# A four-layer attention and Fourier kernel: the feature transform of the spectral layers moved behind the sequence transform, in seven block products instead of eight

## The chip, the cores and the metric

The kernel runs on one core of one Trainium2 chip. The core has a matrix engine (TensorE, in the profile PE, its weight loads PEld), a vector engine (VectorE, DVE), a scalar engine (ScalarE, ACT), a general engine (GpSimd, POOL) and a queue engine that issues most of the transfers (SyncE, SP). Each engine works through its own instructions in order and waits for semaphores of the others. The metric is the time of one execution on the device in microseconds (us), the median of several runs.

## What is computed

Four residual layers over a sequence of 2,048 rows with 640 features, all in float32. Layers 0 and 2 are a local attention (32 heads of 20, each row sees 8 rows, itself and seven earlier ones two apart), layers 1 and 3 are a Fourier mixing whose two transforms are written as products with given matrices.

```python
def _B_ref(x, dft_seq_re, dft_seq_im, dft_hid_re, dft_hid_im):
    a = jnp.einsum("bsd,ed->bse", x, dft_hid_re)
    b = jnp.einsum("bsd,ed->bse", x, dft_hid_im)
    y = jnp.einsum("ts,bse->bte", dft_seq_re, a) - jnp.einsum("ts,bse->bte", dft_seq_im, b)
    return y

x = A_x
x = x + _A_ref(_layernorm(x, axis=-1), A_wqkv, A_wo)
x = x + _B_ref(_layernorm(x, axis=-1), B_dft_seq_re, B_dft_seq_im, B_dft_hid_re, B_dft_hid_im)
x = x + _A_ref(_layernorm(x, axis=-1), A_wqkv, A_wo)
x = x + _B_ref(_layernorm(x, axis=-1), B_dft_seq_re, B_dft_seq_im, B_dft_hid_re, B_dft_hid_im)
```

## The kernel before

**Precision.** Every operand of a matrix product is split in two float32r numbers, high and low, by a copy on ACT and a subtraction on DVE. A product is three passes (`PASSES`: high by high, high by low, low by high) into the same bank of PSUM, the accumulators. There are eight banks of 128 x 512, called `m0`, `m1`, `xt`, `t0`, `t1`, `pq`, `aux0` and `aux1`.

**The spectral layer** (class `LayerB`, line 902) applies the sequence transform first. The 2,048 output rows are eight tiles of 256. For a tile t, z = C x, where C has a real and an imaginary part side by side (512 columns) and x has 640 features: five blocks of 128 features, each one bank. The sequence matrix comes from DRAM in pieces of 128 x 512 ("tables", `cs`, 256 KB), sixteen to a tile, and is split as it comes. Then the feature transform makes y from z (`ymm`, line 1063): for 128 rows, five blocks of features, two halves of 320 output columns, three passes, real and imaginary: 60 products of 320 columns. Its weights, real and negated imaginary, are loaded and split in each spectral layer by `load_w` (line 1000) and stay in SBUF. `yout` (line 1082) adds the residual rows, stores them and, in layer 1, collects the statistics of the next layer's norm.

**Tiles 0 and 1** are made plainly, 15 products of 512 columns a table (`z_mm`, line 981): tile 0 at the end of the attention layer before, tile 1 at the start of the spectral layer (`zpart`, line 1024). Beside tile 1, DVE and ACT form sums and differences of blocks of x (`x_whole`, `x_combine`), which are stored to DRAM (`xcb`).

**Tiles 2 to 7** go in three pairs (`pair`, line 1179). The first 512 features are done by seven block products instead of eight (m1 to m7, each two banks, on sums and differences of quarters of the matrix and of x); the last 128 features plainly (f1, f2, one bank each). A pair takes three sweeps over eight table steps: m5, m4, m7 (18 products of 512 columns a step), then m2, f1, f2, m1 (21), then m3, f2, m6 (15). Each sweep reads its tables from DRAM again and splits them; kept operands of x come back by `x_slot`. Between sweeps DVE and ACT empty the banks and form z. The feature products of the previous tile stand between the sweeps of a pair, 60 at a time, those of the pair's first tile are strewn through the third sweep, 12 a step, and 60 stand after it.

**The way to the next attention layer.** `early` (line 601) runs the last pair of layer 1 with hooks that load, normalise and transpose the first rows of layer 2. The two halves of the last tile's feature products (`prev.ymm`, line 832) stand in steps -3 and -2 of attention's own hand-written order, among the first groups of its query, key and value product (g0 to g15, 15 products of 480 columns each; `LEAD2`, line 47, gives their steps). Keys and values of a group are stored to DRAM (`qkv_store`, line 385) and come back as windows; a query is copied by ACT into PSUM (`q_copy`, line 417); then attention's first product on DVE can start.

**Order.** In the attention layers the order of all engines is written out. In the spectral layers the order of PE alone is; the other engines' order, SP's too, is planned by the framework's scheduler. SP has at most eight transfers outstanding.

Of the kernel before, what the change touches and what calls it, by code (L numbers as in the profile page):

```python
# [20 lines left out]
D = 640  # L21
# [7 lines left out]
NJ = 4  # L29
# [49 lines left out]
XAPART = {(m, i) for i in range(2, NP - 2, 2) for m in (7, 1)}  # L79
# [7 lines left out]
def tile_layers(ctx: ExitStack, tc: tile.TileContext, x, wqkv, wo, cs, wre, wim, out):  # L87
# [29 lines left out]
    for tag, w in (("r1_0", D), ("pr0", D), ("win", SLOTS * FE)):  # L117
        T([P, w], tag, bufs=NWIN if tag == "win" else 1)
# [10 lines left out]
    xcb = [{m: dr.tile([P, NP, 2, 256], F32, name=f"xc_{l}_{m}") for m in XC} for l in range(2)]  # L129
# [126 lines left out]
    def layer_a(li, stats, handoff, prev):  # L256
# [344 lines left out]
        def early():  # L601
# [4 lines left out]
            def w0():  # L606
                with tc.issue_after(prev.dma.ins):
                    wq[0] = a_weights_q(0)

            def xt(j, part, bank="pq"):  # L610
                xt_pe(0, j, part, bank)
                xt_hi(0, j, part)
                xt_lo(0, j, part)

            prev.pair(
                NPAIR - 1,
                stats,
                {
                    2: lambda: (x_get(0), x_get(1)),
                    4: lambda: xt(0, 0),  # L620
                    5: lambda: x_get(2),
                    6: lambda: xt(0, 1),
                    7: lambda: (w0(), xt(1, 0), x_get(3)),
                    ("y", 0): lambda: xt(1, 1),
                    ("y", 1): lambda: (xt(2, 0, "xt"), xt(2, 1, "t0")),
                    ("y", 2): lambda: xt(3, 0),
                    ("y", 3): lambda: xt(3, 1, "xt"),
# [202 lines left out]
        if prev is not None:  # L830
            for j2 in range(2):
                at(j2 - 3, "pe3", prev.ymm, NT - 1, j2, 0, KD)
                at(j2 - 2, "actl", prev.yout, NT - 1, j2, stats)
# [68 lines left out]
    class LayerB:  # L902
        def __init__(self, li):
# [4 lines left out]
            self.zt = {}  # L908
            self.xl, self.raw, self.ct = {}, {}, {}
            self.xc = xcb[li // 2]  # L910
            self.whole = {}
            self.nraw = self.nhl = self.nx = 0

# [86 lines left out]
        def load_w(self):  # L1000
            self.wr = None
            self.wi = [None] * KD
            tags = ("stg", "stg", "xa", "xa")
            for n, (x, k) in enumerate([(x, k) for k in range(KD) for x in "ri"]):
                raw = T([P, D], tags[n] if n < 4 else "xa", bufs=2)
                nc.sync.dma_start(raw, (wim if x == "i" else wre)[:, k, :])
                if x == "i":
                    wt = T([P, 2, D], f"pr{k}" if k < 4 else "zo3", F32R)
                    self.wi[k] = wt[:, 0], wt[:, 1]
                    split(wt[:, 0], wt[:, 1], raw, neg=True)  # L1010
                else:
                    if self.wr is None:
                        self.wr = T([P, 2, KD, D], "r2a", F32R)
                    split(self.wr[:, 0, k], self.wr[:, 1, k], raw)

# [8 lines left out]
        def zpart(self, t, s0, s1):  # L1024
            for s in range(s0, s1):
                self.cw_load(t, s)
                self.c_hl(s, t)
                self.z_mm(s, None, t)

        def zt_new(self, t):  # L1030
            self.tt = [T([P, 5, 256], tg, F32R) for tg in ("zo0", "zo1", "zo2", "ot")]
            self.zt[t] = {}

        def zt_put(self, t, k, z):
            tt, zt = self.tt, self.zt[t]
            loc = [divmod(k * 4 + d, 5) for d in range(4)]
            for d in range(4):
                zt[(k, d // 2, d % 2)] = tt[loc[d][0]][:, loc[d][1]]
            pieces = [[], []]
# [6 lines left out]
            for o, r in pieces[0]:  # L1046
                nc.scalar.copy(o, z[:, r])
# [358 lines left out]
```

## Time and profile before

| | us |
|---|---|
| median of 3 runs | 1756.59 (1749.93 to 1758.09) |
| the profiled execution's own time | 1755.72 |
| its span in the trace | 1753.9 |
| PE busy | 1724.9 |
| DVE busy | 1372.8 |
| ACT busy | 804.9 |
| POOL busy | 627.9 |

The page gives for one execution the busy time of each engine, the span in 40 slices, the transfers, the chain of work that ended last, and the costliest groups of instructions. Views of the trace give groups of instructions by line, instructions in order of time, and busy times of each engine in chosen windows. In a row such as `12.34 0.39 PE L1171 MATMUL t<-r,r 128*128 128x512 f32 x3`, the first number is the start in us from the span's start, the second the time that the merged instructions took, then engine, source line, operation, output and inputs by the program's names, shapes and how many instructions the row merges. Matmuls are pipelined: a single one is shown with 0.3 to 0.4 us, while the next starts earlier, so that paces are read from start to start.

### The profile page before, as it was taken

The numbers are of one execution on the slowest core, as the hardware profiler recorded it, in microseconds if no ns is written. First come the engines' busy times: TensorE is split into PE (matmuls) and PEld (weight loads), VectorE is DVE, ScalarE is ACT, GpSimd is POOL, SyncE is SP. The second block draws the span as 40 slices with busy tenths as digits, with TensorE's granted clock in tenths as the row PEclk, the third lists the DMA queues.
The fourth block names the chain that finished last, engine by engine and source line by source line (L and its number), as shares of the span: only waits on it lengthen the run. The fifth ranks groups of instructions, "written<-read, shape, count | busy, mean of one in ns | idle before, by whom it ended". The sixth has DMA issues, their size and how long they took to land.

```text
span 1753.9 us, 26453 instructions
## 1 busy us (share of the span) xinstructions
PE 1724.9 (98%) x8798; PEld 1502.2 (86%) x8798; DVE 1372.8 (78%) x2127; ACT 804.9 (46%) x1683; POOL 627.9 (36%) x589
## 2 busy tenths in 40 slices
PE   9999999899999999999999999999999999999999
PEld 7888888788888888888898889988788888888888
DVE  6999999988767767767648999989777677677673
ACT  5664543554444444445534434444434443443441
POOL 4899999940000000000028998889200000000000
PEclk9999999999999999999999999999999999999999
DMA  8997769759787777686657866798597867767861
GB/s 285 309 314 217 227 200 335 260 185 313 260 264 243 242 258 231 233 278 221 198 178 237 267 205 214 220 326 278 192 316 254 262 209 253 260 220 237 261 205 53
DMA packets 273961, 426.20 MB, mean 243 GB/s; under 512 B 22656, under 2 KB 153728, under 8 KB 273568
## 3 DMA queue, kind: packets, MB, share of 16 engines
q1 hardware_dynamic: 270624, 422.54, 73.3%
q10 hardware_dynamic: 3200, 1.97, 0.4%
q8 instruction: 70, 1.15, 0.3%
q14 instruction: 67, 0.55, 0.1%
HBM read 339.28 MB, written 85.14 MB: 242 GB/s over the span
## 4 chain that ended last, share of the span: by engine, by line
PE 72%; DVE 11%; DMA 8%; POOL 4%; issue 3%; ACT 1%; SPq 0%; DVEq 0%; ACTq 0%; POOLq 0%
PE m L376 17%; PE aux L1074 14%; PE t L1171 10%; PE m L1171 10%; PE pq L1171 5%; PE xt L1171 5%; PE aux L529 5%; PE m L992 2%; DMA win<-kvb 2%; PE t L992 2%; DVE pr L445 2%; DVE pr L485 2%; DMA xc<-stg 1%; POOL pr L504 1%; DMA win<-cs_in 1%
## 5 line engine op out<-in xcount | busy, mean ns | idle before, releaser
L376 PE MATMUL m<-r,s 128*128 128x480 f32 x1920 | 435.7, 381 | 1.4 <-ACT stg L383 1.0
L376 PEld LDWEIGHTS m<-r,s 128*128 128x128 f32 x1920 | 355.0, 188 | 55.0 <-ACT stg L383 1.8
L1164 ACT CAST r<-win 128x512 fp32r<-128x512 f32 x246 | 149.8, 620 | 168.4 <-DVE win L1200 92.1
L1074 PE MATMUL aux<-r2a,zo 128*128 128x320 f32 x768 | 226.1, 309 | 0.0
L504 POOL TENSOR_TENSOR pr<-pr 128x640 f32<-128x640 f32 x126 | 207.0, 1643 | 33.9 <-DVE pr L485 33.8
L1074 PE MATMUL aux<-pr,zo 128*128 128x320 f32 x704 | 207.8, 309 | 0.0
L188 POOL TENSOR_TENSOR stats<-stats,mhalf 128x1 f32<-128x1 f32 (+1 forms) x40 | 28.5, 712 | 492.3 <-ACT stats L184 483.1
L445 DVE TENSOR_TENSOR pr<-pq,win 128x1280 f32<-128x1280 f32 x128 | 189.8, 1484 | 12.5 <-DMA win<-kvb 7.1
L1165 DVE TENSOR_TENSOR r<-win,r 128x512 fp32r<-128x512 f32 x246 | 165.6, 688 | 43.3 <-ACT r L1164 41.6
L485 DVE TENSOR_TENSOR pr<-pq,win 128x1280 f32<-128x1280 f32 x128 | 190.7, 1491 | 5.1
L448 POOL TENSOR_TENSOR pr<-pr 128x640 f32<-128x640 f32 x117 | 168.5, 1440 | 14.7 <-DVE pr L445 11.8
L1171 PE MATMUL m<-r,r 128*128 128x512 f32 x594 | 151.3, 389 | 0.3 <-DVE r L1165 0.3
L1074 PEld LDWEIGHTS aux<-r2a,zo 128*128 128x128 f32 x768 | 144.1, 188 | 1.9
L1074 PEld LDWEIGHTS aux<-pr,zo 128*128 128x128 f32 x704 | 132.2, 188 | 2.1
L1171 PE MATMUL t<-r,r 128*128 128x512 f32 x498 | 133.5, 390 | 0.0
L1171 PEld LDWEIGHTS m<-r,r 128*128 128x128 f32 x594 | 111.2, 188 | 23.6 <-DVE r L1165 0.9
L992 PE MATMUL m<-s,r 128*128 128x512 f32 x384 | 120.1, 400 | 8.3 <-DMA s<-c0b 5.5
L992 PE MATMUL t<-s,r 128*128 128x512 f32 x384 | 118.1, 396 | 0.2 <-DVE ot L1049 0.2
L455 DVE TENSOR_REDUCE lg<-pr 128x64 f32<-128x640 f32 (+1 forms) x128 | 111.4, 871 | 6.4 <-POOL pr L448 6.1
L505 POOL TENSOR_TENSOR pr<-pr 128x320 f32<-128x320 f32 x126 | 112.2, 890 | 9.9
L1171 PEld LDWEIGHTS t<-r,r 128*128 128x128 f32 x498 | 93.5, 188 | 20.0
L383 ACT COPY stg<-m 128x480 f32<-128x480 f32 x128 | 71.0, 555 | 84.4 <-PE m L376 63.4
(301 smaller groups left out, 3204.8 us busy)
## 6 DMA issues: line engine op xcount, KB each, us to landing
win<-cs_in SPq DMA_DIRECT2D x351, 256.0 KB, 3.8
r<-xc SPq DMA_DIRECT2D x240, 256.0 KB, 4.4
win<-kvb SPq DMA_DIRECT2D x96, 440.0 KB, 4.7
xa<-cs_in SPq DMA_DIRECT2D x121, 256.0 KB, 3.7
win<-kvb SPq DMA_DIRECT2D x64, 360.0 KB, 4.6
kvb<-stg SPq DMA_DIRECT2D x60, 320.0 KB, 5.2
xc<-stg SPq DMA_DIRECT2D x32, 512.0 KB, 4.3
s<-c0b SPq DMA_DIRECT2D x26, 512.0 KB, 5.2
```

Of the source, the lines that this page charges most:

```text
L376: nc.tensor.matmul(mt[g][:, : 3 * F], st[:, a, k], wq[q][:, b, k], start=n == 0, stop=n == 14)
L445: nc.vector.tensor_tensor(pr, q, wview(u, jp, 0, [[1, FE]]), op=ALU.mult)
L448: nc.gpsimd.tensor_tensor(pv[:, :, 0:10], pv[:, :, 0:10], pv[:, :, 10:20], op=ALU.add)
L455: nc.vector.tensor_reduce(lgs[u][:, :, 2 * jp : 2 * jp + 2].rearrange("p h j w -> p (j w) h"), prq.pop((u, jp)), axis=AX.X, op=ALU.add,)
L485: nc.vector.tensor_tensor(pr.rearrange("p j w (h d) -> p j w h d", d=DH), lgs[u][:, :, 2 * jp : 2 * jp + 2].rearrange("p h j w -> p j w h" ...
L504: g.tensor_tensor(pr[:, :, 0:4], pr[:, :, 0:4], pr[:, :, 4:8], op=ALU.add)
L505: g.tensor_tensor(pr[:, :, 0:2], pr[:, :, 0:2], pr[:, :, 2:4], op=ALU.add)
L992: self.last = nc.tensor.matmul(self.z[t][k], self.xn[c][:, a, j, k * P : (k + 1) * P], self.ct[s][:, b], start=s == 0 and i == 0, stop=s = ...
L1074: self.last = nc.tensor.matmul(self.ym[e][:, :320], zt[(k, a, ri)][:, j2 * P : (j2 + 1) * P], w[:, e * 320 : (e + 1) * 320], start=(k, a, ...
L1164: nc.scalar.copy(hi, raw)
L1165: nc.vector.tensor_tensor(lo, raw, hi.bitcast(F32), op=ALU.subtract)
L1171: nc.tensor.matmul(bank, w(a, kb), hl[b], start=start and (a, b) == (0, 0), stop=stop and (a, b) == (1, 0),)
```

## The change

All changes but names and buffers are in the two spectral layers and in the border from the first of them to the second attention layer.

1. **Feature transform last.** No feature product runs between or in the sweeps any more. Each tile's z is stored to DRAM (`zb`), five blocks of 128 x 512 a tile in pieces of 512 bytes, and read back by a last phase, `hid`, that does all eight tiles, two at a time.
2. **Seven block products of eight.** z (real and imaginary) has two by two blocks against the weights, by output half. `hid` forms seven operands from z for each tile (`prep`: 11 operations on DVE and 7 copies on ACT, on 128 x 640), three steps ahead of use, and multiplies each by one of seven operands made from the weights: 15 products of 320 columns an operand and tile, 210 for a pair of tiles in place of 240. Four pairs of banks take them; DVE adds eight bank halves a tile to the residual rows.
3. **Weights.** The seven weight operands are formed and split once, in layer 1's first sweeps (`b_prep`, 20 parts), stored to DRAM (`wbd`, 35 blocks of 320 KB) and read back by each layer's `hid`, as buffers come free: ten into `r2a`, four into `pr0` and `pr1` during the last second sweep, the rest around the start of `hid`.
4. **Two sweeps a pair.** With all eight banks free of feature products, a first sweep has m5, m2, m1, f1, f2 (30 products a step) and a second m3, m6, m4, m7 (24); m4 and m7 accumulate onto m2 and m1 in their banks.
5. **x operands.** Four of the five kinds of operands of x stay in SBUF, two of them written over the blocks of x that they replace; one (m1) goes through DRAM. For that, tile 1's tables are taken in another order.
6. **Border.** The hooks that load, normalise and transpose layer 2's first rows move into `hid`'s last two groups of tiles; attention's steps -3 to -1 hold no feature products.

```diff
-                m5, m4, m7 = banks("m0", "m1"), banks("xt", "t0"), banks("t1", "pq")
+                m5, m2, m1 = banks("aux0", "aux1"), banks("m0", "m1"), banks("t0", "t1")
+                f1, f2 = banks("xt"), banks("pq")
                 for i in range(NP):
...
+                    b22, b11, b21, b12 = raw(t2, NP + i), raw(t1, i), raw(t1, NP + i), raw(t2, i)
+                    x1 = self.x_slot(i)
+                    p22 = split(b22)
+                    self.product(m5, self.x_kept(5, i), p22, *ends)
+                    p11 = split(b11)
+                    self.product(m2, self.x_kept(2, i), p11, i == 0, False)
+                    c1 = comb(b22, b22, b11, ALU.add)
+
+                    self.product(m1, x1, c1, i == 0, False)
+                    self.product(f2, self.x_plain(*k2(i), 512), p22, i == 0, False)
+                    self.product(f1, self.x_plain(*k1(i), 512), p11, i == 0, False)
+                    p12 = split(b12)
+                    self.product(f2, self.x_plain(*k1(i), 512), p12, False, i == NP - 1)
+                    p21 = split(b21)
+                    self.product(f1, self.x_plain(*k2(i), 512), p21, False, i == NP - 1)
...
+                m3, m6 = banks("aux0", "aux1"), banks("pq", "xt")
+                for i in range(NP):
...
+                    c3 = comb(self.s_buf(tags), b12, b22, ALU.subtract)
+                    self.product(m3, self.x_plain(*k1(i), 0), c3, *ends)
+                    c6 = comb(b12, b11, b12, ALU.add)
+                    self.product(m6, self.x_kept(6, i), c6, *ends)
+                    c4 = comb(b11, b21, b11, ALU.subtract)
+                    self.product(m2, self.x_plain(*k2(i), 256), c4, False, i == NP - 1)
+                    c7 = comb(b22, b21, b22, ALU.add)
+                    self.product(m1, self.x_kept(7, i), c7, False, i == NP - 1)
+                    self.flush()
+                    if p == NPAIR - 1:
+                        self.hid_load(i)
...
+        def hid_load(self, i):
+            if i == 0:
+                self.b0 = self.b_tile("r2a", 0, 10)
+            if i in (0, 1, 2, 5, 6):
+                n = (0, 1, 2, None, None, 3, 4)[i]
+                self.b0(2 * n, 2 * n + 2)
+            if i == 4:
+                za = self.za_tile(0)
+                for n in range(2):
+                    za(n, 0, 4)
...
+        def hid_mm(self, t, n, bank, start, stop):
+            s = self.av.pop((t, n))
+            for k in range(KD):
+                w = self.wb[(n, k)]
+                for a, b in PASSES:
+                    nc.tensor.matmul(
+                        bank[:, :320],
+                        s[:, a, k],
+                        w[:, b],
...
+                for step in range(NT // 2 * NB):
+                    g, n = divmod(step, NB)
...
+                    for i, t in enumerate(ts):
+                        self.hid_mm(t, n, bank[which][i], n in (0, 1, 2, 4), n in (1, 2, 5, 6))
...
+                        for q in quarters:
+                            o = rows[(t, q // 2)][:, q % 2 * 320 : q % 2 * 320 + 320]
+                            v.tensor_tensor(o, bank[which][i][:, :320], o, op=ALU.add)
...
+                    self.prep(step + 3)
+                    if (g, n) in hooks:
+                        hooks[(g, n)]()
...
-        if prev is not None:
-            for j2 in range(2):
-                at(j2 - 3, "pe3", prev.ymm, NT - 1, j2, 0, KD)
-                at(j2 - 2, "actl", prev.yout, NT - 1, j2, stats)
```

562 lines of the change are left out of this document (306 added, 256 removed).

## The prediction

> **What bounds the kernel now.** I read the page's busy shares and its chain first, then the busy time by windows, then PE in order of time at both ends of each spectral layer.
>
> ```profile
> span 1753.9 us, 26453 instructions
> PE 1724.9 (98%) x8798; PEld 1502.2 (86%) x8798; DVE 1372.8 (78%) x2127; ACT 804.9 (46%) x1683; POOL 627.9 (36%) x589
> PE 72%; DVE 11%; DMA 8%; POOL 4%; issue 3%; ACT 1%; SPq 0%; DVEq 0%; ACTq 0%; POOLq 0%
> ```
>
> PE is busy nearly always, but a busy share says little about the pace. The windows do (columns: window, length, then busy us and instruction count of PE, PEld, DVE, ACT, POOL, then granted clock, DMA share, GB/s):
>
> ```profile
> 250.00:300.00 50.00, 46.51 (x246) 40.62 (x245) 46.74 (x70) 22.61 (x61) 46.16 (x43) 0.97 0.90 306
> 400.00:450.00 50.00, 49.97 (x248) 42.29 (x247) 39.51 (x59) 20.52 (x37) 0.00 (x0) 1.00 0.91 313
> 850.00:900.00 50.00, 50.00 (x299) 46.76 (x299) 21.93 (x41) 24.58 (x52) 5.04 (x4) 1.00 0.52 162
> 1050.00:1100.00 50.00, 50.00 (x280) 45.46 (x279) 45.95 (x72) 22.16 (x57) 45.08 (x43) 1.00 0.68 220
> 1150.00:1200.00 50.00, 46.64 (x245) 40.48 (x245) 43.13 (x67) 22.30 (x58) 44.49 (x43) 0.97 0.97 339
> 1400.00:1450.00 50.00, 50.00 (x256) 43.74 (x255) 37.53 (x63) 22.11 (x38) 0.00 (x0) 1.00 0.66 213
> ```
>
> In the spectral layers (400, 1400) POOL rests, DVE has 10 to 12 us of every 50 free, and PE has none. There the end is set by the number of products. In the attention layers (250, 1050) DVE and POOL are as full as PE. So this change is worth what it does to PE inside the spectral layers, and at their borders. The prices of a product come from start to start, since a product's own duration overlaps the next:
>
> ```profile
> 725.08 8.79 PE aux L1074 x60
> ...
> 1693.42 1.52 PE L1171 MATMUL m<-s,r 128*128 128x512 f32 x6
> 1694.78 0.39 PE L1171 MATMUL xt<-r,r 128*128 128x512 f32 x1
> ```
>
> Sixty feature products of 320 columns take 8.79 us on the chain, 0.1465 each. Six sequence products of 512 columns take 1694.78 - 1693.42 = 1.36 us, 0.2267 each.
>
> ```profile
> 401.30 0.30 PE L1074 MATMUL aux<-r2a,zo 128*128 128x320 f32 x1
> ...
> 902.50 7.76 PE L376 MATMUL m<-r,s 128*128 128x480 f32 x35
> ...
> 1272.60 0.30 PE L1074 MATMUL aux<-r2a,zo 128*128 128x320 f32 x1
> ...
> 1750.33 0.31 PE L1074 MATMUL aux<-zo,ot 128*128 128x320 f32 x1
> ```
>
> 401.30 and 1272.60 are the first feature products of the layers; four tables of tile 1 (60 products, 13.6 us) stand ahead of them, so tile 1 starts at 387.7 and 1259.0. The first layer's last feature product ends as group g5 of the next attention begins, 902.50. Its PE work: 1,536 sequence products (348.2), 960 feature products (140.6), five groups (some 16.5) and 20 transposes (some 2): 507 of 514.8 us, so about 7.5 idle. Layer two: 348.2 + 140.6 = 488.8 of 1750.5 - 1259.0 = 491.5, under 3 idle.
>
> **The change, part by part.** *Feature products.* Seven block products of eight: per pair of tiles 7 x 2 x 15 = 210 instead of 240, per layer 840 instead of 960. Removed: 240 x 0.1465 = **35.2 us**, all on the path. Same width and passes, so I take the same pace. *Sequence sweeps.* Products stay 54 per table step (18 + 21 + 15 before, 30 + 24 after): no gain. Input loads fall, 216 to 192 table loads and 120 to 24 loads of kept operands a layer. The two x halves rewritten in place wait for PE's last table, and ACT evacuates five banks behind that: by the next rows some five copies at 0.62, of which two to three products cover half. Bounds 0 and 4, I take 2.
>
> ```profile
> L1164 ACT CAST r<-win 128x512 fp32r<-128x512 f32 x246 | 149.8, 620 | 168.4 <-DVE win L1200 92.1
> L1165 DVE TENSOR_TENSOR r<-win,r 128x512 fp32r<-128x512 f32 x246 | 165.6, 688 | 43.3 <-ACT r L1164 41.6
> ...
> 1681.13 0.68 DVE L1265 TENSOR_TENSOR s<-m,s 128x512 f32<-128x512 f32 x1
> 1681.73 0.68 DVE L1266 TENSOR_TENSOR stg<-stg,xt 128x512 f32<-128x512 f32 x1
> ```
>
> *Borders of sweeps.* Before, 60 feature products (8.79) or products strewn through the third sweep covered the emptying of banks. After, five borders a layer stand bare. DVE's operations on 512 columns follow each other at 0.60 (1681.13 to 1681.73). The first product into a reused bank comes 18 products (4.1 us) after its last use in most cases, more than four DVE additions (2.4). In the built order one border of the first layer has six such operations ahead of a half that PE needs 1.4 us later: 3.6 - 1.4 = 2.2. Bounds 0 and 11 (2.2 at all five); I take 1 a layer.
>
> *Second sweep.* Eight DVE operations a step (four combinations, four low halves): 8 x 0.60 = 4.8 us against PE's 24 x 0.2267 = 5.44. Cost nothing, covered by 0.6 us a step and by up to eight halves of lead; the rival below prices it without.
>
> *Hand-over to the feature products.* In the last second sweep SP also loads 14 weight blocks and two tiles of z back from DRAM, 22 x 320 KB = 7.2 MB, beside 20 table pieces (5.2 MB) for steps 2 to 6: 12.4 MB. The row at 1150 moves 339 GB/s at a share of 0.97, so 37 us, and from the point where the first weight buffer is free to step 6 PE has about 38 us. But the z loads (1.3 MB each) can only start when PE has left the first x quarter after step 3, two steps (10.9 us) ahead of step 6; they take 2.6 MB / 339 = 7.7 us and a landing of some 3 to 4:
>
> ```profile
> win<-cs_in SPq DMA_DIRECT2D x351, 256.0 KB, 3.8
> ```
>
> Behind them stand step 6's tables, and on DVE the first feature operand's halves (which wait for the z) stand ahead of step 5's last two and of step 6. Tables at about 12.5, then combination, high and low half (0.6 + 0.6 + 0.7 and hand-offs): 14.5 to 15 against 10.9, so **4 us**; bounds 0 (if the z land as fast as a short load, 3.8) and 8 (if they move at the 213 GB/s of the 1400 row, 12.3 us). After the sweep 7.5 MB more must land in six feature steps of 4.4 us: 22 us of 26. I take 1.5 (0 and 6). Small single waits, as the second layer has now: 1.5. Together 2 + 1 + 4 + 1.5 + 1.5 = **10 us a layer**.
>
> *Feature phase.* DVE per group of two tiles: 22 operations on 640 columns (some 0.75, scaled from 0.60 at 512) and 16 additions on 320 (some 0.4): 23 us against PE's 210 x 0.1465 = 30.8. Operands are made three steps ahead. Hidden; without the lead the fullest step (6 us) would cost 1.6 four times a layer. Its row loads wait for row stores on the same SP queue, with eight to ten us to spare.
>
> *The last tile's feature products leave the next attention's start.* They covered, with g4, the way of the first keys through DRAM:
>
> ```profile
> 881.86 0.56 ACT L383 COPY stg<-m 128x480 f32<-128x480 f32 x1 [0.35 <-PE m L376]
> 882.46 0.36 ACTq L392 DMA_DIRECT2D kvb<-stg  x1
> ...
> 905.15 0.42 ACT L418 COPY pq<-qs 128x320 f32<-128x320 f32 x1
> ...
> 908.23 1.48 DVE L445 TENSOR_TENSOR pr<-pq,win 128x1280 f32<-128x1280 f32 x1
> ...
> 890.46 3.41 PE L376 MATMUL m<-r,s 128*128 128x480 f32 x15
> ...
> kvb<-stg ACTq DMA_DIRECT2D x4, 320.0 KB, 2.7
> ...
> win<-kvb SPq DMA_DIRECT2D x96, 440.0 KB, 4.7
> ```
>
> Now from g3's copy (881.86) to attention's first product on DVE (908.23) 26 us pass, since ACT's query copy (905.15) stands behind the last tile's statistics. After: four groups (13.6), copy 0.6, store 3.1, load 4.7, and 3 for issue and queueing: DVE starts 25 us after the last feature product (bounds 22 and 30). PE has by then done g0 to g6 in both versions, so the rest of the attention layer is the same. The weight quarters of q come in one at a time through the one free window buffer, while four hold result rows; the last is due just at the end, within the bound.
>
> **The sum.** First layer from tile 1's start to attention's first DVE product: before 908.2 - 387.7 = 520.5; after 348.2 + 840 x 0.1465 (123.1) + 2 + 10 + 25 = 508.3: -12.2. Second layer to the last product: before 491.5, after 471.3 + 10 = 481.3: -10.2. The tail (last product to end, 3.4) has the same add and store. Total -22.4 from the profiled execution's 1755.7: 1733.3; that execution is 0.9 below the median of the runs, so **1734 us**.
>
> **Rivals.** *All covers hold* (waits of 2 a layer): 1734 - 16 = 1718. For it: layer two now idles under 3 us. Against: bare borders. *Clock*: where PE idled 3.5 us in 50 (250) or 3.4 (1150), the clock stood at 0.97, a further 1.5 us; 24 us of waits in such lumps would lose 24 / 3.5 x 1.5 = 10: 1744. Against: they are mostly short. The Trainium skill, "TensorE: Matmul & The Clock Gate", Part 1, says an idle window of about 3.4 us halves PE's clock until a busy one has passed; by that rule only the hand-over and the attention's start would pay, and the trace agrees as far as 0.97 beside those idle times goes. *The change doesn't reach the end at the first layer*: the attention's start takes back its 12 us because keys or weights come late: 1746. *Transfers late, the slower side*: place the hand-over. At 220 GB/s (the row at 1050) 12.4 MB take 56 us, 18 late, and 7.5 MB take 34, 8 late: 26 a layer for the 5.5 counted, +41: 1775. It decides from about 11 us a layer, near 250 GB/s; the mean is 243 with free time in it, full-share rows give 313 to 349, which speaks against. Stores of z in 512-byte pieces, which no row has, push this way. *Second sweep bound by DVE*: operations at 0.69 plus 0.18 of waiting for ACT (43.3 / 246) make 6.9 us a step against 5.44, 11.7 a sweep, 9 behind the lead, six sweeps: 1734 + 54 = 1788. Against: 0.60 back to back.
>
> **Chances.** Forecast 0.58 (own range 1722 to 1748); covers hold 0.10; clock 0.08; first layer lost 0.06; transfers late 0.12; DVE 0.06. Half a per cent, about what can be told from no change, is 8.8 us: faster means below 1747.8. Forecast 0.56, covers 0.10, clock 0.06, first layer 0.04: 0.76. Within: 0.11 (edges, and transfers a little late). Slower: 0.13. The range 1720 to 1758 leaves out half of the covers case, DVE, and most of late transfers, about 0.2.
>
> **What would show it.** Feature products 1,680 at 0.146 to 0.147 start to start; gaps of some 4 us in each layer's last second sweep ended by DVE or a z load; under 2.5 us at sweep borders; attention's first DVE product 22 to 30 us after the last feature product. Waits over 11 us a layer, or a second sweep step over 5.9 us, would make the prediction wrong.

## The result and the profile after

| | before | after |
|---|---|---|
| median of 4 runs, us | 1753.26 (1749.12 to 1758.09) | 1728.87 (1725.96 to 1730.85) |
| profiled execution's own time | 1755.72 | 1728.94 |
| its span | 1753.9 | 1727.1 |

The ratio of the times is 0.9859, with an interval of 0.9824 to 0.9893. Forecast were 1734 us and a range of 1720 to 1758. The page of the changed kernel:

```profile
span 1727.1 us, 25610 instructions
PE 1690.0 (98%) x8558; PEld 1465.1 (85%) x8558; DVE 1439.9 (83%) x2215; ACT 828.0 (48%) x1677; POOL 629.6 (36%) x589
PE 52%; DVE 21%; DMA 12%; POOL 7%; issue 4%; ACT 3%; SPq 1%; ACTq 0%; DVEq 0%; POOLq 0%
```

PE has 240 products and 34.9 busy us less (1724.9 - 1690.0), DVE 67 us more. In the chain DVE rises from 11 to 21% and transfers from 8 to 12%: PE still sets the end, but more often on the word of another. Where, the windows show (columns as before):

```profile
450.00:500.00 50.00, 47.90 (x210) 39.38 (x211) 40.62 (x68) 26.99 (x50) 0.00 (x0) 1.00 0.87 303
500.00:550.00 50.00, 46.86 (x198) 36.10 (x196) 45.65 (x78) 23.65 (x42) 0.00 (x0) 1.00 0.87 287
700.00:750.00 50.00, 47.04 (x198) 37.77 (x197) 40.12 (x66) 22.64 (x38) 0.00 (x0) 0.97 0.86 305
1400.00:1450.00 50.00, 50.00 (x223) 41.40 (x222) 34.16 (x56) 23.94 (x41) 0.00 (x0) 1.00 0.69 221
1550.00:1600.00 50.00, 47.09 (x202) 37.14 (x201) 40.70 (x66) 22.48 (x37) 0.00 (x0) 1.00 0.83 300
```

At 0.2267 a product, 50 us hold 220. Layer two's middle (1400) has them. Layer one lacks 10 to 22 in three of these windows, layer two 18 in its last one, and in all four the transfers are at 0.83 or more.

The ends of the stages, in PE's and DVE's instructions in order of time (tile 1's first product in each spectral layer, the last feature products, attention's first product on DVE), first after, then the one row of before that the prediction had only worked back:

```profile
386.54 1.30 PE L990 MATMUL m<-s,r 128*128 128x512 f32 x5
...
874.77 2.22 PE L1358 MATMUL m<-r,ot 128*128 128x320 f32 x14
...
901.66 1.49 DVE L447 TENSOR_TENSOR pr<-pq,win 128x1280 f32<-128x1280 f32 x1
...
1245.44 1.29 PE L990 MATMUL m<-s,r 128*128 128x512 f32 x5
...
1721.61 2.36 PE L1358 MATMUL m<-r,ot 128*128 128x320 f32 x15
```

```profile
1257.72 0.96 PE L992 MATMUL m<-s,r 128*128 128x512 f32 x3 [1.45 <-DVE zo L1049]
```

The first layer's last feature product ends at 874.77 + 14 x 0.1467 = 876.8, the second's at 1721.61 + 15 x 0.1467 = 1723.8. Stage by stage, in us (before's first layer starts at 387.3 by its trace):

| stage | before | after | difference | forecast |
|---|---|---|---|---|
| up to tile 1 of layer one | 387.3 | 386.5 | -0.8 | 0 |
| tile 1 to attention's first DVE product | 520.9 | 515.1 | -5.8 | -12.2 |
| second attention layer, to tile 1 of layer two | 349.5 | 343.8 | -5.7 | 0 |
| tile 1 of layer two to the last product | 492.8 | 478.4 | -14.4 | -10.2 |
| tail | 3.4 | 3.3 | -0.1 | 0 |
| sum | | | -26.8 | -22.4 |

So the time came out within 5 us of the forecast, but its parts did not: the first layer gained half of what was said, and something that the change doesn't touch gained as much as that layer. Of the 5 us, 3 lie in the reference: the forecast took 1756.6 us for before, the median of three runs, and with a fourth run it is 1753.3. As a difference of medians the gain is 24.4 us, where 22.6 were forecast.

### The profile page after: what moved, and what is told of

It reads as the page before. It is cut to its first block, busy times and chain, and to the rows that moved or that the text cites. A ratio compares the mean times of both kernels' runs of the same rounds, so it can differ in the third digit from the quotient of the medians.

```text
span 1727.1 us, 25610 instructions
## 1 busy us (share of the span) xinstructions
PE 1690.0 (98%) x8558; PEld 1465.1 (85%) x8558; DVE 1439.9 (83%) x2215; ACT 828.0 (48%) x1677; POOL 629.6 (36%) x589
## 4 chain that ended last, share of the span: by engine, by line
PE 52%; DVE 21%; DMA 12%; POOL 7%; issue 4%; ACT 3%; SPq 1%; ACTq 0%; DVEq 0%; POOLq 0%
PE m L378 10%; PE aux L1125 4%; PE t L1125 4%; DVE pr L447 4%; PE m L1125 4%; PE m L1358 4%; PE aux L1358 3%; PE m L990 3%; PE t L1358 3%; PE t L990 3%; DVE pr L487 3%; PE pq L1125 3%; PE xt L1125 3%; PE aux L531 3%; POOL pr L506 2%
## 5 line engine op out<-in xcount | busy, mean ns | idle before, releaser
L450 POOL TENSOR_TENSOR pr<-pr 128x640 f32<-128x640 f32 x117 | 168.4, 1440 | 14.2 <-DVE pr L447 13.4
L990 PEld LDWEIGHTS t<-s,r 128*128 128x128 f32 x384 | 72.4, 189 | 15.8 <-ACT r L366 0.5
L531 PE MATMUL aux<-r2a,ot 128*128 128x320 f32 x540 | 84.9, 310 | 0.7 <-ACT s L366 0.5
L990 PEld LDWEIGHTS m<-s,r 128*128 128x128 f32 x384 | 71.6, 189 | 16.3 <-DMA s<-c0b 2.4
L465 ACT ACTIVATE lg<-lg 128x128 f32<-128x128 f32 x64 | 20.1, 314 | 134.5 <-DVE lg L476 134.2
L531 PEld LDWEIGHTS aux<-r2a,ot 128*128 128x128 f32 x540 | 81.2, 188 | 2.8 <-ACT s L366 0.7
L990 PE MATMUL xt<-s,r 128*128 128x512 f32 x192 | 72.5, 391 | 0.0
L508 POOL TENSOR_TENSOR zo<-pr 128x160 f32<-128x160 f32 x126 | 68.1, 540 | 9.9
L1114 ACT CAST zo<-win 128x512 fp32r<-128x512 f32 x83 | 51.4, 621 | 28.5 <-DVE win L1119 13.6
L1115 DVE TENSOR_TENSOR zo<-win,zo 128x512 fp32r<-128x512 f32 x83 | 57.0, 687 | 7.6 <-ACT zo L1114 7.5
L420 ACT COPY pq<-qs 128x320 f32<-128x320 f32 x64 | 27.5, 430 | 70.5 <-DVE pr L487 48.7
```

The source lines that it names most:

```text
L450: nc.gpsimd.tensor_tensor(pv[:, :, 0:10], pv[:, :, 0:10], pv[:, :, 10:20], op=ALU.add)
L531: nc.tensor.matmul(m[:, :320], oT[(c, j)][:, a, k], wo_s["w"][:, b, k, e * 320 : (e + 1) * 320], start=(i, k) == (0, 0), stop=(i, k) == (2 ...
L990: self.last = nc.tensor.matmul(self.z[t][k], self.xn[c][:, a, j, k * P : (k + 1) * P], self.ct[s][:, b], start=s == 0 and i == 0, stop=s = ...
```

## Where the first layer's gain went, as the trace shows it

Of the first layer's 490.3 us (386.54 to 876.8), 471.3 are products by the prediction's prices and some 2 transposes: 17 are lost, for 10 forecast. Of the second's 478.4, 7.1 are lost. The feature phase itself is as forecast:

```profile
1657.81 4.56 PE L1358 MATMUL m<-r,s 128*128 128x320 f32 x30
1662.21 2.36 PE L1358 MATMUL aux<-r2a,s 128*128 128x320 f32 x15
```

4.40 / 30 = 0.1467 a product. Some 12 of the first layer's 17 us stand at three places (2.3, 4.4 and 5.1 us); the rest are losses of 1.1 us or less, at the second pair's middle, in the second sweeps and in tile 1. First, the middle of the first pair, between its two sweeps (rows of ACT, PE, SP and DVE in order of time; the bracket is the idle time ahead and what ended it):

```profile
497.37 0.74 ACT L142 ACTIVATE pr<-pr 128x640 fp32r<-128x640 f32 x1 [2.54 <-DMA wbd<-pr]
...
499.04 0.57 ACT L1248 COPY zo<-pq 128x512 f32<-128x512 f32 x1
...
499.67 0.96 PE L1125 MATMUL pq<-stg,r 128*128 128x512 f32 x3 [2.10 <-ACT zo L1248]
...
493.87 0.41 SPq L1103 DMA_DIRECT2D win<-cs_in  x1
499.64 0.52 SPq L1013 DMA_DIRECT2D zb<-zo  x1
...
505.94 0.38 SPq L1103 DMA_DIRECT2D xa<-cs_in  x1
...
511.33 0.69 DVE L1119 TENSOR_TENSOR win<-win,xa 128x512 f32<-128x512 f32 x1 [4.19 <-DMA xa<-cs_in]
```

An operation that forms the feature weights (L142) waits on ACT for the store of the block before it, and the bank copy that PE needs (L1248) stands behind it: 2.1 us on PE. SP stands from 493.87 to 499.64 at the store of that same copy, with tables behind it. A table of the second sweep is issued at 505.94, and DVE idles 4.19 us for it. From 511 on DVE runs without a gap: eight operations of 0.60 in a step of 5.44, and besides them, up to the border, eight operations of forming that take 4.2 us. Of a sweep's 43.5 us (eight steps) DVE so has about 1 free (43.5 - 64 x 0.60 - 4.2). Second, 30 us later, at the border to the next pair (PE):

```profile
540.76 0.39 PE L1125 MATMUL m<-zo,r 128*128 128x512 f32 x1
541.99 0.93 PE L1125 MATMUL aux<-e,r2a 128*128 128x512 f32 x3 [0.84 <-DVE s L1269]
544.39 0.94 PE L1125 MATMUL aux<-e,r2a 128*128 128x512 f32 x3 [1.47 <-DVE s L1269]
...
551.24 0.96 PE L1125 MATMUL t<-zo,xr 128*128 128x512 f32 x3 [0.24 <-DVE s L1277]
```

From 540.76 to 551.24 stand 27 products, worth 6.12: 4.4 us lost. The prediction had 2.2 at one border of this layer, which it doesn't name. Third, two steps into the last second sweep (SP, DVE, PE, and the busy times of ten us ahead of it and of four behind it):

```profile
697.42 0.80 SPq L1285 DMA_DIRECT2D r2a<-wbd  x2
...
700.32 0.92 SPq L1285 DMA_DIRECT2D r2a<-wbd  x2
...
704.18 0.34 SPq L1103 DMA_DIRECT2D e<-cs_in  x1
...
714.50 0.69 DVE L1119 TENSOR_TENSOR e<-e,win 128x512 f32<-128x512 f32 x1 [9.00 <-DMA e<-cs_in]
...
715.95 0.51 PE L1125 MATMUL aux<-stg,r 128*128 128x512 f32 x1 [2.24 <-ACT stg L1114]
717.18 2.32 PE L1125 MATMUL aux<-stg,r 128*128 128x512 f32 x5 [0.72 <-DVE stg L1115]
719.30 1.48 PE L1125 MATMUL pq<-ot,r 128*128 128x512 f32 x3
```

```profile
700.00:710.00 10.00, 10.00 (x46) 8.29 (x45) 5.50 (x10) 3.98 (x7) 0.00 (x0) 1.00 1.01 377
...
717.00:721.00 4.00, 3.82 (x10) 3.00 (x11) 4.00 (x8) 1.72 (x4) 0.00 (x0) 0.57 0.60 177
```

From 697.42 to 700.32 SP issues six transfers of two weight blocks each (640 KB, 3.8 MB). The transfers run at full share (1.01, 377 GB/s), and the table issued at 704.18 behind them reaches DVE 10.3 us later, where the page's medians for loads of a table are 3.1 to 4.1. PE waits 2.24 and 0.72, and then runs at half clock: five products take 2.12 us (717.18 to 719.30), not 1.13. Some 5 of the second layer's 7.1 us are lost in its last steps, in several waits of under 1 us, of which one is shown with what DVE did before it:

```profile
1564.99 0.69 DVE L1119 TENSOR_TENSOR win<-win,e 128x512 f32<-128x512 f32 x1 [6.90 <-DMA e<-cs_in]
...
1580.39 1.56 DVE L1331 TENSOR_TENSOR r<-r,r 128x640 fp32r<-128x640 f32 x2 [1.94 <-ACT r L1330]
...
1587.68 1.43 PE L1125 MATMUL aux<-pr,r 128*128 128x512 f32 x5 [0.72 <-DVE pr L1115]
```

Here DVE has the same late table (6.90), and then the first feature operand's halves (L1331), which wait for a load of z.

From this a theory: PE's waits in the sweeps are late tables, which DVE at 88% of a step (4.8 of 5.44) can't make up before the border. Against it stood the order at the border, the forming of weights, the number of buffers and the sheer bytes.

## The experiments

All are edits of the changed kernel. "Of before" is the ratio to the kernel before, run beside it (its median was 1751.8 to 1754.3). The last four columns are spans in the profiled execution: layer one from tile 1's first to the last feature product, from there to attention's first DVE product (the lead-in), from there to tile 1 of layer two, and layer two to its last product.

| run | median us (runs) | of before | layer one | lead-in | attention | layer two |
|---|---|---|---|---|---|---|
| changed kernel | 1728.87 (4) | 0.9859 | 490.3 | 24.8 | 343.8 | 478.4 |
| e1_again | 1729.16 (4) | 0.9863 | 490.4 | 25.6 | 344.1 | 477.6 |
| e2_no_forming | 1726.69 (4) | 0.9845 | 485.5 | 25.2 | 345.4 | 478.0 |
| e3_eight_views | 1727.85 (4) | 0.9855 | 486.9 | 24.5 | 344.2 | 480.1 |
| e4_eight_products | 1766.63 (4) | 1.0073 | 507.2 | 24.2 | 347.4 | 494.7 |
| e5_weights_spaced | 1724.08 (4) | 0.9839 | 485.2 | 25.1 | 345.9 | 475.8 |
| e6_first_quarter_first | 1730.34 (4) | 0.9876 | 491.0 | 26.7 | 344.0 | 477.3 |
| e7_one_order | 1734.16 (4) | 0.9896 | 492.7 | 24.6 | 345.2 | 478.9 |
| e8_forming_on_pool | 1747.83 (10) | 0.9969 | 507.5 | 24.0 | 344.7 | 478.1 |
| e9_stores_later | 1725.49 (4) | 0.9848 | 485.6 | 25.6 | 346.4 | 477.7 |
| e10_one_addition_fewer | 1723.48 (4) | 0.9825 | 482.8 | 25.4 | 347.5 | 480.3 |
| e11_before_again | 1754.89 (1) |  | 517.1 | 5.7 | 345.7 | 494.1 |
| e12_three_mended | 1723.84 (5) | 0.9826 | 485.8 | 24.3 | 345.3 | 477.5 |

The next table divides PE's lost time in layer one among its places, in us. It is the time of each stretch from start to start, less its products at 0.2267 and 0.1467. The border is cut a little wider than in the rows above (4.8 for 4.4), and the last column has some 2 of transposes in it.

| run | middle of pair one | its second sweep | border to pair two | pair two | border to pair three | last second sweep and feature phase |
|---|---|---|---|---|---|---|
| changed kernel | 2.4 | 1.2 | 4.8 | 1.7 | 0.6 | 7.4 |
| e1_again | 1.5 | 1.2 | 4.9 | 0.9 | 0.6 | 8.4 |
| e3_eight_views | 2.4 | 0.5 | 4.7 | 0.1 | 0.6 | 6.5 |
| e2_no_forming | 0 | 1.1 | 5.1 | 0 | 0.6 | 6.7 |
| e5_weights_spaced | 1.8 | 0.6 | 4.7 | 0 | 0.1 | 5.2 |
| e8_forming_on_pool | 2.8 | 3.3 | 5.3 | 14.2 | 2.1 | 7.6 |
| e9_stores_later | 2.7 | 0 | 1.6 | 0 | 1.7 | 7.1 |
| e10_one_addition_fewer | 2.0 | 0 | 1.4 | 0.4 | 0 | 6.9 |
| e12_three_mended | 0 | 0.5 | 3.2 | 0.3 | 3.4 | 6.4 |

The first three rows have the same layer one, since e3 edits layer two alone: the places differ by up to 2 us by chance, the border to pair two by 0.2 only.

**The two kernels again.** No edit.

> The changed kernel again, unaltered, to see which waits come back. If the waits read from its first trace are set by the order of work, they return at the same places: in the first spectral layer some 8 us at sweep borders (of which 2.3 at the first border of the first pair and 3.8 at the border between the first two pairs) and some 5 us two steps into the last second sweep; in the second spectral layer none at borders and some 4 us in the last steps of its last second sweep. If they are chance, they move or change by more than half. The 5 us that the third layer's attention was shorter than before is expected not to be the change's: its part near the wait for a kept table operand may be absent in another run. Time 1729, within 5.

> The kernel before, a second trace. From its first to the changed kernel the second attention layer (from attention's first DVE product to tile 1's first sequence product of the second spectral layer) shrank from 349.5 to 343.8 us, which the change doesn't touch; in the changed kernel's runs it has been 343.8 to 347.4. If that is chance of the first trace (a wait for a kept table operand, with half a clock behind it), this trace shows 343 to 346; if the change brings it, 348 to 351.

The changed kernel's waits came back at the same places; layer one lost 17.1 us again. The second trace of the kernel before has 345.7 for the attention layer that had 349.5, inside the 343.8 to 347.5 of the changed kernel's variants: the attention's 5.7 us are mostly chance of one trace, not the change.

**The price of a product.**

```diff
                 w = self.wb[(n, k)]
+                for r in range(2 if n == 6 else 1):
...
-                        stop=stop and (k, a, b) == (KD - 1, 1, 0),
+                            stop=stop and (k, a, b) == (KD - 1, 1, 0) and (n, r) != (6, 0),
```

> The seventh block product of each tile is done twice, so that there are again eight for each tile, 960 feature products a layer (the sum is not the reference's). If every feature product lies on the path at 0.1465 us, the time rises by 240 x 0.1465 = 35 us to 1764, half of it in each layer. Rival (part of it is hidden, because PE waits in the feature phase or at the start of the next attention anyway): it rises by 28 or less. If the first layer's part is hidden by the lead-in of the attention, only the second layer's 17.6 shows.

Layer one grew by 16.9 us and layer two by 16.3 (507.2 - 490.3, 494.7 - 478.4), the lead-in stayed. The feature phase alone, from the end of the sweeps to the last product, grew by 17.3 and 17.6, in sum 34.9; of the 38 between the spans, 5 lie in the attention layers, which differ as much from run to run. So the 35 us that the change removes lay on the path in full, in both layers.

**Forming and buffers.** In e2 `b_prep` stores the loaded weights in place of formed ones. In e3:

```diff
-            if self.li == 3:
-                views += [("pr2", 1), ("pr3", 1)]
```

> Leaves out the forming of the feature weights (the ACT and DVE operations of b_prep); its loads and stores stay, so the stored blocks are the plain weights. Theory (forming is what fills DVE in the first layer's sweeps, so that what a border needs comes late): the first layer's border waits of some 8 us fall below 2.5, the wait two steps into the last second sweep stays at some 5, and the time falls by 4 to 8 to about 1723. Rival (the borders of the first layer wait because its operands have 8 buffers where the second layer's have 10, or because of the order at the border itself): border waits stay within 2 of 8 and the time stays at 1729.

> The second spectral layer's table operands get 8 buffers as in the first layer, not 10. Theory (forming): the second layer's borders stay below 2 us in sum, time within 2 of 1729. Rival (buffers): waits of 5 to 9 us appear at the second layer's borders, and the time rises to 1734 to 1738.

Without forming the middle borders of layer one's first two pairs have no wait, as expected, but the border between the first two pairs still has its own (PE and DVE of e2):

```profile
547.53 1.80 PE L1125 MATMUL t<-zo,xr 128*128 128x512 f32 x5 [2.40 <-DVE s L1254]
...
522.46 0.69 DVE L1119 TENSOR_TENSOR win<-xa,win 128x512 f32<-128x512 f32 x1 [3.11 <-DMA win<-cs_in]
```

DVE is late here with no forming on it, and behind a late table again. So forming explains the middle borders (ACT's queue, not DVE's load). At the other nothing was gained (5.1 us lost for 4.8): the theory written ahead of the run fell for that border. With eight buffers layer two got no wait at its borders; but the burst of weights now reached PE there too, as in layer one:

```profile
1565.27 0.50 PE L1125 MATMUL aux<-zo,r 128*128 128x512 f32 x1 [1.18 <-ACT zo L1114]
```

Two more operand buffers are what hid the 6.90 us of 1564.99 in layer two.

**The order at the border.** The three pairs share one region of written order:

```diff
-            for p in range(NPAIR):
-                self.pair(p)
+            with tc.manual_schedule(engines={nc.tensor.engine}):
+                for p in range(NPAIR):
+                    self.pair(p)
```

> The written order of PE's products spans all three pairs, so that the scheduler can't move products of the next pair forward. In the changed kernel six products of the second pair's first step stand ahead of the last 17 of the first pair in the first layer, so that PE asks for two banks 17 products (3.9 us) sooner than DVE has emptied them. Theory (this order makes the wait at that border): the 3.8 to 4.1 us there (with half clock up to 5.5) fall below 1; nothing else changes; time 1725. Rival (DVE is late by itself, since the forming of weights and the border's own operations meet): at least 2.5 us stay.

The theory fell. The wait only moved: with the six products gone from there, PE stands at the next product of its own pair, which needs a low half from DVE (L1115). It also grew, with the clock at half behind it (PE's row, then the busy times):

```profile
545.64 2.50 PE L1125 MATMUL m<-zo,r 128*128 128x512 f32 x5 [3.50 <-DVE zo L1115]
```

```profile
545.60:550.00 4.40, 4.36 (x10) 3.51 (x11) 4.40 (x9) 2.05 (x4) 0.00 (x0) 0.50 1.02 344
```

DVE is late by itself. The six products that the scheduler had moved forward filled part of the wait rather than made it.

**Does DVE lack the slack to recover?**

```diff
-                    c7 = comb(b22, b21, b22, ALU.add)
+                    c7 = split(b22)
```

> In the second sweeps one of the four table combinations is left out (its operand is split as loaded; the result is not the reference's), so DVE has 7 operations a step, 4.2 us of 5.44, not 8. PE, its order and the transfers stay. Theory (PE's waits at the ends of second sweeps are a late table that DVE can't make up at 0.6 us a step; with 1.2 a step a lag of 4 us is gone in four steps): the border between the first layer's first two pairs falls from 3.8-5.2 to below 1, the second layer's waits in its last second sweep from 4 to below 2.5, and the time by 4 to 8. Rival (the border's own six operations make the wait, however early DVE is): at least 2.5 us stay at that border.

PE's row at that border, and DVE's in the second layer's last sweep:

```profile
545.60 1.66 PE L1125 MATMUL m<-stg,r2a 128*128 128x512 f32 x6 [0.49 <-ACT s L1274]
...
1579.77 1.56 DVE L1331 TENSOR_TENSOR r<-r,r 128x640 fp32r<-128x640 f32 x2 [2.51 <-ACT r L1330]
```

DVE idled 4.2 us near 512 here too (for a forming operation whose weights landed late), yet PE lost only 0.65 and 0.41 at two products of the border, 1.4 in all and not 4.8: the lag had been won back. Below 1 was expected, and 2.5 or more by the rival. Layer one is the shortest of all, 482.8, and the median fell by 5.4, as expected. The second layer is the miss: its last sweep got worse, with DVE standing at the halves that wait for z. There slack doesn't help; the wait is the prediction's own, an operation on a late load of z in DVE's queue.

**What makes the tables late.** In e9 the stores of a second sweep are issued behind the tables of its fourth step, in e5 the weight blocks behind the tables of their own step:

```diff
-                    self.flush()
+                    if i > 2:
+                        with tc.issue_after(self.tab.ins):
+                            self.flush()
```

```diff
                     if p == NPAIR - 1:
-                        self.hid_load(i)
+                        with tc.issue_after(self.tab.ins):
+                            self.hid_load(i)
```

> In the second sweeps the stores that stand on SP's queue (two copies of a finished quarter of z, and formed weights) are queued behind the tables of the fourth step, no longer behind those of the first. Theory (a table for the sweep's third step comes late because the queue stands behind a store that waits for ACT's bank copy; DVE then waits 3 to 4 us for it and can't make it up, at 8 operations of 0.60 in a step of 5.44, so that PE meets it at the border): DVE's wait for a table near the start of the first layer's first second sweep falls from 4.2 (changed kernel) to below 2, and the 3.8 to 5.2 us at the border behind it to below 2; time some 3 less, 1726. Rival (the table waits for its buffer or for other transfers): DVE's wait stays over 3 and so does the border.

> The weight blocks that the last second sweep loads are queued on SP behind the tables of the step that asks for them, instead of all at its start. Theory (in the first layer some 3.8 MB of weight blocks issued within 4 us stand ahead of the tables of the sweep's third step, whose first table lands 10 us after its issue; PE waits 3.4 us and then runs 4 us at half clock): that wait of some 5.4 us with its half-clock products falls below 1.5, and the time falls by some 4. Rival (the sweep moves too many bytes in all, wherever they stand): the same 5 us appears later in the sweep or at the start of the feature phase, the sum of the layer's waits stays within 1.5 of 15.

In e9 no table is late at that place; DVE waits 2.25 us for a forming operation, and PE's border has one wait left (DVE, then PE):

```profile
509.83 0.49 DVE L1154 TENSOR_TENSOR pr<-pr,pr 128x320 fp32r<-128x320 f32 x1 [2.25 <-ACT pr L1153]
...
546.09 1.96 PE L1125 MATMUL t<-zo,xr 128*128 128x512 f32 x6 [0.39 <-DVE s L1279]
```

PE does 25 products, worth 5.67, from 540.67 to 547.89: 1.6 us lost, not 4.4 to 4.8, which is far outside what this border varies by chance. Layer one falls by 4.7. The rest of that is in the sweep ahead of the border and in pair two, where the three traces of the unedited layer differ by nearly as much; the border to pair three loses 1.1 more, and the last sweep as much as before, though its clock stays up. The middle border still loses some 2.5, since ACT's queue is as before. In e5 DVE's waits for the table behind the weight blocks fall from 9.00 to 3.79 and, in layer two, from 6.90 to 2.00, and PE passes the place in layer one without a gap:

```profile
706.42 0.69 DVE L1119 TENSOR_TENSOR e<-e,win 128x512 f32<-128x512 f32 x1 [3.79 <-DMA e<-cs_in]
...
1557.63 0.69 DVE L1119 TENSOR_TENSOR win<-win,e 128x512 f32<-128x512 f32 x1 [2.00 <-DMA e<-cs_in]
```

Layer one falls by 5.1 and layer two by 2.6, for the same bytes. So the late table of both places was a matter of what stands ahead of it on one queue. But the rival, that the sweep moves too much, was half right. PE loses 2.0 at 733 and 1.5 at the start of the feature phase and in it instead, so that the last sweep and the feature phase fall by 2.2 only (7.4 to 5.2; the unedited layer has 6.5 to 8.4). The other 3 us of layer one are at places that the edit doesn't touch.

**The quarter of z that is needed first.**

```diff
-                for n in range(2):
-                    za(n, 0, 4)
+                for a, b in ((0, 1), (1, 4)):
+                    for n in range(2):
+                        za(n, a, b)
```

> The two tiles of z that the last second sweep loads back come in two pieces each, the quarter that the first feature operand needs ahead of the rest. Theory (the prediction's: DVE's halves for that operand wait for a z load of 1.3 MB and stand ahead of the last steps' tables): the second layer's 4 us in its last two sweep steps fall to 2 or less; in the first layer, where the earlier wait lets the loads catch up, no change. Rival (the wait is set by the bytes, or by the tables that stand behind the z loads on SP): it stays within 1 of 4.

Inconclusive: DVE's wait for ACT's copy of z fell from 1.94 to 1.06 us, and layer two by 1.1, no more than e1 differs from the first trace (0.8).

**Forming on POOL, which rests.** `b_prep`'s copies and subtractions on POOL.

> The forming of the feature weights runs on POOL, which rests in the spectral layers, and no more on ACT and DVE. Theory (at the first sweeps' ends ACT stands in a forming operation that waits for the store of the block before it, 2.5 us in the changed kernel, with the two bank copies behind it): the 1.4 to 2.3 us at the first pair's middle border and the 0.6 to 1.0 at the second's go, and the border between the first two pairs stays at 3 to 4; sum of the first layer 11 to 12 instead of 15, time 1726. Rival (POOL's operations slow DVE's): DVE's operations on 512 columns in the first layer's sweeps come out over 0.72 instead of 0.68 and the layer gains nothing or loses.

The rival held, and layer one lost 17 us. The same 43 operations of DVE, in the changed kernel and here:

```profile
L1115 DVE TENSOR_TENSOR zo<-win,zo 128x512 fp32r<-128x512 f32 x43 | 29.5, 687 | 0.8 <-ACT zo L1114 0.7
```

```profile
L1115 DVE TENSOR_TENSOR zo<-win,zo 128x512 fp32r<-128x512 f32 x43 | 33.7, 785 | 1.0 <-ACT zo L1114 0.9
```

687 ns became 785. At eight operations a step, 0.1 us more each takes all of the 0.6 that DVE had to spare. But most of the 17 us stands at one place, in pair two (rows of POOL, SP, DVE and PE):

```profile
626.87 13.11 POOL L1170 TENSOR_TENSOR pr<-pr 128x320 f32<-128x320 f32 x1 [6.84 <-DMA wbd<-pr]
...
644.33 0.33 SPq L1156 DMA_DIRECT2D wbd<-pr  x1
...
650.50 1.26 DVE L1119 TENSOR_TENSOR e<-win,win 128x512 f32<-128x512 f32 x1 [11.27 <-DMA win<-cs_in]
...
652.43 2.50 PE L1125 MATMUL m<-stg,r 128*128 128x512 f32 x5 [6.62 <-DVE stg L1115]
```

One forming subtraction takes 13.11 us, where the four others of its line take 0.96 to 1.38. It ends at 639.98, just after DVE's unbroken row of operations, at 639.24. The Trainium skill, "SBUF — State Buffer", section "Who interferes with whom", says that a DVE operation with two inputs in SBUF and a POOL operation that reads SBUF shut each other out for a whole instruction; the rows agree. SP, which issued its last table at 631.44, stands until 644.33 at the store of what POOL forms, with tables behind it. DVE waits 11.27 us for one of them, and PE 6.62, with half clock behind it: 9.7 us lost. So by the trace it is once more a store at the head of the queue, and what is left for the slower operations is the smaller part.

**Three mends together.** The edits of e5 and e9, and the last two forming operations of the first two pairs behind the bank copies on ACT:

```diff
-                    nc.scalar.copy(fr[:, n], f[0])
+                    cp = nc.scalar.copy(fr[:, n], f[0])
...
+                if self.bprep and p < 2:
+                    with tc.issue_after(cp.ins):
+                        for _ in range(2):
+                            next(self.bprep, None)
```

> Three mends together, the result is whole: the last second sweep's weight blocks behind the tables of the step that asks for them (as in the run with spaced weights), the stores of the second sweeps behind the tables of their fourth step (as in the run with later stores), and in the first two pairs the last two forming operations put on ACT behind the two bank copies of the middle border. If the first layer's waits are these three places (5.3 two steps into the last second sweep with half clock, 3.8 to 5.2 at the border of the first two pairs, 2.3 and 0.9 at the middle borders), its waits fall from 15 to 4 to 7, the second layer's from 6 to 4 to 5, and the time to 1717 to 1721. Rival (what is mended in one place comes back in the next, since DVE and the transfers have little slack in the second sweeps): 1724 to 1726, as each mend alone.

1723.84 us (1721.30 to 1726.81), 0.9826 of before (0.9807 to 0.9845): below both kernels by its median, but its interval overlaps the changed kernel's, and it can't be told from the weights alone (1724.08; 0.9839, 0.9801 to 0.9876). The rival held. The middle borders lost their waits, and two others came up behind them (PE, second border between pairs):

```profile
642.90 0.92 PE L1125 MATMUL aux<-zo,r2a 128*128 128x512 f32 x3 [0.86 <-DVE s L1276]
...
646.55 0.73 PE L1125 MATMUL t<-stg,xr 128*128 128x512 f32 x2 [1.37 <-DVE s L1284]
```

Of the forming that was moved out of the way, 5.0 us of DVE now fall into pair two's second sweep, where the changed kernel has 0.7; DVE has no room for them. e9 has 4.2 there, and loses 1.7 at the same border. The last sweep and the feature phase lost 6.4 all the same, 4.0 of it at 731 to 738 with half clock, and the border to pair two 3.2, twice what e9 left there. Why these two came back was not tried.

## Why the prediction was right, and where it was not

- *Feature products, 35.2 us.* Right: 0.1467 start to start, and putting 240 back costs 34.9 in the feature phases.
- *Lead-in, 25 us (22 to 30).* Right: 24.8, and 24.0 to 26.7 in all variants. It didn't change when 120 products were put ahead of it (e4), as the sum assumed.
- *Tail.* Right: 3.3 for 3.4.
- *Hand-over, 4 us a layer by halves that wait for z.* Right in size, and in layer two in kind (1.94 us at L1331, e10; the try at mending it, e6, settled nothing). In layer one the loss came 25 us sooner, by weight blocks ahead of tables. The sum of bytes over the whole sweep, from which the term was made, could not show a burst within it; that layer two has the same burst and survives it by two buffers, the prediction had not looked at.
- *Sweep borders, 1 us a layer.* Wrong for layer one, right for layer two (none). The border between the first two pairs lost 4.4 to 4.9, where 2.2 was said for the worst one, and the operations that stand there were the smaller part: with DVE's lag of 30 us earlier mended (e9) or won back (e10), 1.4 to 1.6 stayed.
- *Second sweep, nothing.* This is the step that failed: "covered by 0.6 us a step and by up to eight halves of lead". The pace of 0.60 was right; but a lead is spent once, by the first late table, and 0.6 a step needs seven steps to give 4 us back. The term also left out the forming, of which 4.2 us fall into the first pair's second sweep. The forecast had this as a rival (DVE sets the step), with slower operations as its condition; it needed no slower operations.
- *Waits of 10 us a layer.* 17 and 7.1: 24 in sum where 20 were said. That the sum is close is luck, for the errors have different causes.
- *The rest of the attention layer is the same.* Right by the second trace of before, within 1.9 us. With that trace in place of the first, the first layer up to attention gained 7.7 us (522.8 to 515.1) for 12.2 forecast, and layer two 15.7 (494.1 to 478.4) for 10.2. That the two errors nearly cancel, and so the time comes out near the forecast, is luck too.
- *Layer two, -10.2.* It was -14.4: 2.9 by fewer waits (7.1 for 10), and 1.3 because the prediction had worked tile 1's start back to 1259.0, where the trace has 1257.7 and short waits behind it.
- *Clock.* The rival came true in small: in the changed kernel's spectral layers, one stretch near 717 (0.57 over four us).
- *Transfers late at the hand-over.* The rival's place was right, its reason (the mean rate) not: the rate was 377 GB/s at full share there, and order alone took the wait away, though part of it came back later in the sweep (e5).

## What to carry to other kernels

An engine that fills 88% of a step is covered only until its first late input; ask for each sweep what stands on the queue ahead of its first inputs, above all stores that wait for another engine and bulk loads for later. Work that is moved to a resting engine still has its results to store, and can cost more than it frees. And before a few microseconds of one stage are explained, a second trace of the same kernel tells whether they are there.

## What the runs showed of the hardware

PE's clock fell to half after waits of 2 to 3 us in sum, and not always. In the changed kernel, waits of 0.84 and 1.47 us (541.99, 544.39 above) left the clock alone: the next three products took 0.78 us, to 545.17. In e1 the same two waits halved it:

```profile
543.24 1.62 PE L1125 MATMUL aux<-e,r2a 128*128 128x512 f32 x3 [1.47 <-DVE s L1269]
544.66 2.12 PE L1125 MATMUL m<-zo,r 128*128 128x512 f32 x5
```

Three products took 1.42 us. In the clock records of the traces each stretch at half clock inside the spectral layers lasts 3.41 us, or two or three times that: 3.41 at 717 in the changed kernel, 6.83 at 545 in e7, 10.24 at 648 in e8. The Trainium skill, "TensorE: Matmul & The Clock Gate", Part 1, says that the gate watches a free-running window of about 3.4 us; the lengths and the changing outcome agree with that. But a wait as long as the window was not needed: 2.24 and 0.72 us around one product were enough at 717. In the spectral layers six to fifteen products went at half clock each time, 1.5 to 3.0 us beside the wait itself.
